# Gated linear attention and a spatial-gating MLP on one core: a new order table, constants as separate operations, more choice of engine

## The chip, the cores and the metric

The kernel runs on one NeuronCore of a Trainium2 chip. A core has a matrix engine (PE, with its weight loads shown as PEld), a vector engine (DVE), a scalar engine (ACT), a general engine (POOL), and a sync engine (SP) that here issues nearly all DMAs. Each engine takes its instructions strictly in the order in which they were written for it, and waits at semaphores for the others. The metric is the device time of one execution in microseconds.

## The reference

```python
def _attn_ref(q, k, v, alpha):                 # each (4, 8, 768, 48)
    state = np.zeros((B, H, D, D)); y = np.zeros_like(q)
    for t in range(S):
        state = alpha[:, :, t, :, None] * state + np.einsum('bhd,bhe->bhde', k[:, :, t], v[:, :, t])
        y[:, :, t] = np.einsum('bhd,bhde->bhe', q[:, :, t], state)

def _moe_ref(x, w_in, w_spatial, b_spatial, w_out):   # x (4, 768, 384)
    h = np.maximum(x @ w_in, 0.0)                     # 384 -> 1024
    u, v = h[..., :512], h[..., 512:]
    v_n = (v - mean(v)) / np.sqrt(var(v) + 1e-06)     # over the last axis
    v_s = np.einsum('ts,bsd->btd', w_spatial, v_n) + b_spatial[None, :, None]
    return (u * v_s) @ w_out                          # 512 -> 384
```

A recurrence over 768 steps for 4 x 8 heads, and behind it an MLP whose gate mixes the 768 positions. All inputs and the output are fp32.

## The kernel before, in words

**The recurrence in chunks.** The 768 steps of each of 4 batch rows are cut into 6 chunks of 128, 24 chunks in all, numbered i = 0 to 23. In a chunk the recurrence becomes matmuls: the logarithm of alpha (`ln`, written to the tile `la`) is summed along time by a matmul with a triangle of ones (`cum`), exponentials of the sum and of its negative (`eexp`, `einv`) scale q and k (`qt`, `kt`), both are transposed on PE (`trk`) and copied out of PSUM (`ev`, tile `kqT`), scores are a matmul (`sc`), masked on DVE (`m`, tile `ptm`), and the output `y` is the masked scores times v (cast to bf16 by `vb`) plus q times the state so far. The state is carried by `upd` (a matmul), `z` (added on DVE), `S` (scaled on POOL) and `sb` (cast to bf16). Chunks 0 to 7 are handled as four pairs, j = 0 to 3, with the same steps under the names `lnp`, `cump`, `einvp`, `eexpp`, `ktp`, `qtp`, `vbp`, `tr`, `updq`, `ya`; a pair's loads are 384 KB each, a single chunk's 192 KB. Then y is cast (`xs`), transposed (`xt`) and copied into `xT` (`xe`).

**The MLP.** For each batch row: `v` (24 groups of three 512-column matmuls, with ReLU on ACT), statistics (`bn`, `rs`) and the normalised `vn`; `u` (32 groups of three 384-column matmuls); `s`, the spatial mixing (32 groups of six, in two parts `mm/0` and `mm/1`), whose copy out of PSUM on DVE adds the bias (`vsb`); `g`, the product with u on POOL or DVE; `o`, the output projection (four matmuls of 384 columns), its copy on ACT, and the store `st`. The last `o` is cut into two column halves (`oh`). The weights come in over 768 KB loads (`w_in/1`, `w_in/0`, `w_sp/0..2`, `w_out`) and are cast to bf16; w_spatial is transposed on PE (`wt`, copied out by `we`). The bias row is spread over 128 partitions by a matmul with a row of ones (`bb`, copied out by `be` into `bsp_bc`). The very last `s` group adds its bias inside the accumulation instead, by a one-row matmul (L957 to L959).

**What sets the order.** Each step is an `Op` with its engine or a choice of engines. Nothing is scheduled at build time: the table `PLAN` (L57) is a list of words such as `D46`, an engine letter and the number of an op, and `replay` (L111) emits the ops in that order. As every engine is a queue in program order, the table fixes each engine's sequence and, where an op allows several engines, which one does it.

**Filler.** A word such as `P53:512:512:192` also orders matmuls on a tile of constants, `junk`, of so many columns each, into the next PSUM bank, just ahead of op 53 on PE (L185 to L189). Their results are overwritten. Each shows as two matmul records. The table of before holds 1,216 columns ahead of the first `cump`, then 464, 304, 304, 172, 148, 228, 240 and 196 up to the first `u` group, and 300 ahead of `wt/2`.

**Constants.** Triangles, masks, the identity, and zeroed paddings of the operand tiles are made by four ops: `consts` (L238 to L265, listed under POOL, though its memsets run on DVE too) and `cz` 0 to 2 (L267). DVE's first instruction is the memset of `junk`; POOL's first is the DMA of the bias row (L1101), then the triangles `le_pair` and `lt_pair`, the identity, and the mask `mask2`. `mask4` and `ut_ones` come later.

**Loads.** SP issues in the table's order: ac/0, kc/0, qc/0, ac/2, vc/0, kc/2, qc/2, vc/2, ac/4, w_in/1, kc/4, qc/4, vc/4, w_in/0, and so on (`ac` is alpha, the number the first chunk). Three pair-sized buffers for each tensor let loads run ahead. Two stores stand ahead of the last load in this queue, the rest behind.

The lines that the steps below touch are in the functions printed here.

Of the kernel before, what the change touches and what calls it, by code (L numbers as in the profile page):

```python
# [36 lines left out]
class Slot:  # L37
# [5 lines left out]
    "kt": {"POOL": 0.9},  # L43
    "vb": {"POOL": 0.48, "ACT": 0.42},
# [6 lines left out]
    "o": {"ACT": 0.4},  # L51
# [6 lines left out]
S34 Q35 S36 Q37 G32 G0 Q33 S38 Q39 S94 Q95 S40 Q41 A42 P53:512:512:192 A54 D1 D2 D56 P43 S96 Q97 S98 Q99 S100 Q101  # L58
S163 Q164 S4 Q5 S165 Q166 S167 Q168 P59:464 G58 G48 A44 A45 A55 D46 D57 D47 P249:304 P49 P61 A50 P51 D52 D60 A62 A102
A250 P71:304 P74 P113 P103 D72 D73 D76 D75 P63 P77:172 D65 A114 D116 P119:148 A104 A64 A115 A105 A78 G66 G67 G106 D107  # L60
D117 D68 P79 P81 P111 P121 P247 P109 G3 G69 A108 A82 A80 D120 D122 D112 D110 P83 A84 A171 D248 S169 Q170 S9 Q10 S307
Q308 P131 P134 D133 D136 D132 D135 G70 G118 P172:228 P182 P123:240 A183 A8 A173 A124 P137 P138 A139 A174 G7 G6 D125
P85 G126 D128 D185 G127 G129 G175 P88 P142 P140 A86 A184 D176 D186 A143 A89 P188 P190 P180 P144 P178 A141 A191 A145
A181 P146 G11 G12 S309 Q310 S311 Q312 D130 D87 D179 D90 D189 P157 A187 A177 A158 A147 A13 P197 P200 P192 D199 D201
D198 D194 D202 P151:196 P155 A315 A193 A91 P326 P316 A327 P203 P153 P204 G195 G196 G329 A317 A328 A318 P149 A205 A154
D159 D156 D152 D330 G319 P208 P334 A209 P206 D320 P332 P324 P210 P322 D92 D335 D325 D333 D148 A207 P212 A211 A150 P347
P215 P221 A213 A160 A222 A216 S14 Q15 P223 P227 S18 Q19 D93 D323 D161 D348 D349 D214 G16 G17 A224 A228 P225 P229 A226
A21 P232 A234 D231 D230 D233 G20 P235:300 P238 S313 Q314 G331 G321 P344 P336 S367 Q368 S369 Q370 S22 Q23 S371 Q372
A237 A236 D217 D162 D346 A240 D338 A239 A218 D219 D220 A375 A337 P251 P263 P259 P376 A377 A378 G339 P264 D345 D341
D265 P260 D261 P255 P252 A380 A25 A24 D381 D253 P256 D257 G340 G342 G379 S409 Q410 S373 Q374 S446 Q447 S411 Q412 S413  # L70
Q414 S415 Q416 S26 Q27 S480 Q481 S448 Q449 S482 Q483 S450 Q451 S484 Q485 P383 A385 A417 S452 Q453 S577 Q578 S486 Q487
S581 Q582 S579 Q580 S583 Q584 P244 P241 P350 A246 D384 D245 D242 D243 P390 P354 P418 D392 D391 A351 A355 G262 G343
A420 A382 G254 G266 P279 P352 P271 P356 P393 P272 A353 A357 A419 G421 A422 A394 P280 P361 P386 P275 P395 A362 A424
A396 A31 D273 D423 D281 D387 P425 D397 D427 D426 D363 G282 G388 P276 P358 D277 P398 G258 G389 G278 G30 A399 A454 A359
A28 A488 P405 P432 P267 P455 P401 A402 A457 A456 D29 P291 P489 P268 A490 A459 D406 D433 D400 D434 D360 P283 P428 D269
D460 A492 D429 D493 G458 G491 P435 A284 A292 A436 G274 G461 G270 G430 G431 S648 Q649 S617 Q618 S650 Q651 S611 Q612
S652 Q653 S613 Q614 S690 Q691 S615 Q616 S694 Q695 S654 Q655 S692 Q693 P287 P462 P437 P495 P403 D463 D464 D497 D496
# [46 lines left out]
def kernel(  # L124
# [12 lines left out]
    nc = tc.nc  # L137
# [93 lines left out]
    def zero_padding(t):  # L231
# [3 lines left out]
        if t.shape[2] > H:  # L235
            nc.vector.memset(flat[:, :, 0::3, 0:D // 2], 0.0)

    def constants(_):  # L238

        nc.vector.memset(junk, 0.5)  # L240
        nc.gpsimd.memset(le_pair, 0.0)
        nc.vector.memset(mask2[:, 0].bitcast(FP32), 0.0)
        zero_padding(lap_bufs[0])
        nc.vector.memset(ones_col, 1.0)
        nc.vector.memset(halves_of, 0.0)
# [911 lines left out]
```

## Time and profile before

| what | value |
|---|---|
| median of 3 runs | 143.13 us (143.12 to 143.7) |
| the profiled execution | 143.08 us |
| its span, first to last instruction | 141.3 us |
| busy: PE, DVE, ACT, POOL | 133.2, 118.3, 108.6, 83.4 us |
| filler on `junk`, all its records | 10.2 us in 24 records |
| DMA | 28.64 MB, mean 203 GB/s |

The span is what the profiler sees between the first and the last instruction; the execution's own time is 1.8 us longer. The busy time of an engine counts its records, which for PE include the filler. A view by stretch cuts the span and gives each engine's busy time in each piece. A view in order of time gives start, length, engine, line, operation, and in brackets how long the engine sat idle before it and who released it. Groups gather instructions of one line and shape, with the mean length of one.

### The profile page before, as it was taken

What the parts mean: (1) busy time and instruction counts of PE and PEld (TensorE: products, weight loads), DVE (VectorE), ACT (ScalarE), POOL (GpSimd) and SP (SyncE); (2) the same over time, 40 slices, a digit from 0 to 9 for tenths busy, and PEclk for the clock granted to TensorE, in tenths of its full rate; (3) what the DMA queues carried; (4) which work ended last, traced back from release to release, by engine and by line L of the source; (5) the groups of instructions that cost most, each with busy time, mean ns of one, the idle gap of its engine ahead of it and who ended that gap; (6) DMA issues with size and microseconds to landing.
All of it is one profiled execution on the core that took longest, in us unless ns stands there. A gap on an engine that the chain in (4) does not pass through costs nothing.

```text
span 141.3 us, 4968 instructions
## 1 busy us (share of the span) xinstructions
PE 133.2 (94%) x1912; PEld 84.2 (60%) x1923; DVE 118.3 (84%) x291; ACT 108.6 (77%) x282; POOL 83.4 (59%) x146
## 2 busy tenths in 40 slices
PE   7989798999999999999999999999999989999990
PEld 3457575575667656565675665656666656566560
DVE  7479878999989599999998898989979779894940
ACT  3677569988989969889887999997889969940061
POOL 6722986293449596982299899500799993000720
PEclk9999999999999999999999999999999999999999
DMA  4999999999898989989799999979978690112044
GB/s 102 323 323 332 331 272 311 225 320 238 241 232 156 283 161 208 205 161 212 154 205 179 193 217 177 222 143 195 250 151 203 225 375 24 70 56 102 0 164 170
DMA packets 89000, 28.64 MB, mean 203 GB/s; under 512 B 83728, under 2 KB 87440, under 8 KB 88976
## 3 DMA queue, kind: packets, MB, share of 16 engines
q1 hardware_dynamic: 88944, 28.32, 81.6%
q8 instruction: 15, 0.25, 0.7%
q14 instruction: 9, 0.07, 0.2%
q0 software_dynamic: 32, 0.00, 0.0%
HBM read 23.60 MB, written 4.72 MB: 200 GB/s over the span
## 4 chain that ended last, share of the span: by engine, by line
PE 71%; DVE 9%; POOL 7%; issue 5%; ACT 4%; ACTq 0%; POOLq 0%; DVEq 0%
PE bank L828 47%; PE bank L187 4%; DVE ptm L594 3%; PE bank L719 2%; PE bank L754 2%; POOL sbd L199 2%; POOL gT L989 2%; PE bank L511 2%; PE bank L782 2%; DVE ptm L765 2%; PE bank L740 1%; PE bank L583 1%; POOL kt L690 1%; PE bank L666 1%; DVE kqT L199 1%
## 5 line engine op out<-in xcount | busy, mean ns | idle before, releaser
L828 PE MATMUL bank<-w_spT,vn 128*128 128x384 bf16 x192 | 36.8, 326 | 0.0
L989 POOL TENSOR_TENSOR gT<-vsb,uT 128x384 bf16<-128x384 f32 x28 | 25.7, 923 | 14.9 <-DVE vsb L976 14.4
L690 POOL TENSOR_TENSOR kt<-kc,binv 128x384 bf16<-128x384 f32 x16 | 14.6, 914 | 13.4 <-ACT bc L685 8.6
L765 DVE TENSOR_TENSOR ptm<-bank,mask 128x512 bf16<-128x512 f32 x32 | 20.7, 682 | 1.9 <-PE bank L398 1.2
L828 PEld LDWEIGHTS <-vn 128*128 128x128 bf16 x192 | 16.6, 97 | 9.5 <-issue 0.2
L976 DVE TENSOR_TENSOR vsb<-bank,bsp_bc 128x384 f32<-128x384 f32 x31 | 16.5, 551 | 4.2 <-PE bank L828 2.5
L828 PE MATMUL bank<-xT,w_in 128*128 128x384 bf16 x96 | 18.7, 326 | 0.0
L828 PE MATMUL bank<-w_out_sb,gT 128*128 128x384 bf16 (+1 forms) x100 | 18.7, 319 | 0.0
L828 PE MATMUL bank<-w_in,xT 128*128 128x512 bf16 x61 | 17.2, 379 | 0.8 <-issue 0.2
L344 POOL TENSOR_TENSOR state<-state,bc 128x192 f32<-128x192 f32 x20 | 10.4, 520 | 11.4 <-DVE state L337 5.4
L197 ACT COPY kqT<-bank 128x512 bf16<-128x512 bf16 x21 | 12.1, 599 | 3.9 <-PE bank L719 1.1
L199 POOL CAST sbd<-state 64x192 bf16<-64x192 f32 x38 | 13.3, 350 | 2.0
L893 DVE BATCH_NORM_STATS2 stats<-v_sb 128x6 f32<-128x512 bf16 x20 | 13.7, 683 | 0.3 <-ACT v_sb L203 0.3
L203 ACT ACTIVATE v_sb<-bank 128x512 bf16<-128x512 f32 x20 | 11.8, 605 | 1.4 <-PE bank L828 1.3
L197 ACT CAST x_sb<-bank 128x384 bf16<-128x384 f32 x24 | 11.4, 490 | 1.5 <-PE bank L623 1.3
L828 PEld LDWEIGHTS <-w_in 128*128 128x128 bf16 x96 | 8.8, 97 | 5.9
L828 PEld LDWEIGHTS <-gT 128*128 128x128 bf16 x100 | 8.9, 97 | 5.6 <-DVE gT L989 0.4
L199 DVE COPY kqT<-bank 128x512 bf16<-128x512 bf16 x27 | 10.5, 416 | 1.9 <-PE bank L511 1.0
L187 PE MATMUL bank<-junk 128*128 128x512 f32 (+9 forms) x24 | 10.2, 529 | 1.1 <-DVE junk L240 1.1
L594 DVE TENSOR_TENSOR ptm<-bank,mask 128x512 bf16<-128x512 f32 x16 | 10.2, 683 | 0.5 <-PE bank L583 0.4
L197 ACT COPY xT<-bank 128x192 bf16<-128x192 bf16 (+1 forms) x26 | 9.4, 379 | 1.6 <-PE bank L398 1.1
L197 ACT COPY o_sb<-bank 128x384 f32<-128x384 f32 x9 | 4.4, 484 | 8.0 <-PE bank L828 8.0
(126 smaller groups left out, 284.0 us busy)
## 6 DMA issues: line engine op xcount, KB each, us to landing
ac<-in_alpha_dram SPq DMA_DIRECT2D x16, 192.0 KB, 4.1
kc<-in_k_dram SPq DMA_DIRECT2D x16, 192.0 KB, 4.8
qc<-in_q_dram SPq DMA_DIRECT2D x16, 192.0 KB, 4.1
vc<-in_v_dram SPq DMA_DIRECT2D x16, 192.0 KB, 3.8
raw_w<-in_moe_w_spatial_dram SPq DMA_DIRECT2D x3, 768.0 KB, 6.8
out_dram<-raw_w SPq DMA_DIRECT2D x11, 192.0 KB, 2.5
out_dram<-o_sb SPq DMA_DIRECT2D x9, 192.0 KB, 1.8
ac<-in_alpha_dram SPq DMA_DIRECT2D x4, 384.0 KB, 5.0
```

The lines of the kernel that those rows point to most:

```text
L187: nc.tensor.matmul(out=flat[:, 0:cols].rearrange("p (a b) -> p a b", a=4), lhsT=junk, rhs=junk[:, None, 0:n].to_broadcast([128, 4, n]), st ...
L197: nc.scalar.copy(out=out, in_=in_)
L199: ENG[eng].tensor_copy(out=out, in_=in_)
L203: nc.scalar.activation(out=out, in_=in_, func=AF.Relu)
L344: ENG[eng].tensor_tensor(out=st["state"], in0=st["state"], in1=st["bc"][:, :, None].to_broadcast([128, HP, D]), op=ALU.mult)
L594: nc.vector.tensor_tensor(out=st[f"ptm{par}"][:, s], in0=st[f"pt{s}{par}"], in1=mask2[:, par], op=ALU.mult)
L690: ENG[eng].tensor_mul(out=k_blocks(kt3)[:, :, :, 0:D], in0=quad(st["kc"]), in1=st["binv"])
L765: nc.vector.tensor_tensor(out=st["ptm"][:, s], in0=st[f"pt{s}"], in1=mask4, op=ALU.mult)
L828: return lambda ps: nc.tensor.matmul(out=out(ps), lhsT=lhsT(), rhs=rhs(), start=start, stop=stop)
L893: nc.vector.bn_stats(out=stats, in_=d["v_sb"][:, tt, :])
L976: nc.vector.tensor_tensor(out=hold["vs"], in0=ps[:, 0:TH], in1=bsp_bc[:, th, :], op=ALU.add)
L989: ENG[eng].tensor_tensor(out=bt[b]["gT"][:, dsl, cols], in0=hold["vs"], in1=bt[b]["uT"][:, dsl, cols], op=ALU.mult)
```

## The change

The order table is replaced as a whole. Around it:

- The four constant ops become separate ones (`c_junk`, `c_la`, `c_kt`, `c_qt`, `c_col`, `c_ut`, `c_id`, `c_m4`, `c_sbd`, `c_row`, `c_half`, `c_tri`, `c_mz`, `c_m2`), each a dependency of the steps that read it. The same tiles are filled by the same kinds of instruction.
- More ops may run on DVE: `kt`, `vb`, `vbp`, `o`, `xs`, and every `g`.
- The last `s` group's bias is added by a matmul of the identity with `bsp_bc`, 128 rows instead of one.

```diff
 ENGINES = {
-    "kt": {"POOL": 0.9},
-    "vb": {"POOL": 0.48, "ACT": 0.42},
+    "kt": {"POOL": 0.9, "DVE": 0.47},
+    "vb": {"POOL": 0.48, "ACT": 0.42, "DVE": 0.27},
...
-    "o": {"ACT": 0.4},
+    "o": {"ACT": 0.4, "DVE": 0.47},
 }
...
 PLAN = """
-S34 Q35 S36 Q37 G32 G0 Q33 S38 Q39 S94 Q95 S40 Q41 A42 P53:512:512:192 A54 D1 D2 D56 P43 S96 Q97 S98 Q99 S100 Q101
-S163 Q164 S4 Q5 S165 Q166 S167 Q168 P59:464 G58 G48 A44 A45 A55 D46 D57 D47 P249:304 P49 P61 A50 P51 D52 D60 A62 A102
...
+S49 Q50 D7 G10 D6 D4 S109 Q110 D3 D15 S51 Q52 D17 G47 Q48 D12 S111 Q112 D0 D2 G16 D5 D13 D1 G9 D11 S53 Q54 A57 G14
+P264:512:512:192 S113 Q114 P68 A265 P58 A117 P262 S55 Q56 D263 A59 P128:436 A69 D61 A60 G71 S115 Q116 P64:512:512:48
+A70 P118 A65 P74 A129 S178 Q179 D72 A119 G131 D62 A130 P76:512:512:204 D75 A77 P66 S19 Q20 G121 D132 A120 D67 D122 G18
+P86:512:512:436 S184 Q185 A63 P136 D88 P134 A73 P126 P124 D87 A137 P89 S182 Q183 A135 D125 P78 D90 A127 D91 S180 Q181
...
+A160 G144 D204 A196 G28 P172 D163 A194 G145 P207 A173 D102 A27 P212 P215 D209 A26 D217 A208 A330 P164:512:480 S33 Q34
...
 """
...
-        op(("xs", i), "ACT", 0.38, xs, got(("y", i), ("xt", i - WK)), prio=P + 9, use=[st["sl_y"]])
+        op(("xs", i), {"ACT": 0.38, "DVE": 0.47}, None, xs, got(("y", i), ("xt", i - WK)), prio=P + 9, use=[st["sl_y"]])
...
-            lambda ps: ps[:, 0:TH], lambda: ones_row, lambda: b_sp_sb[:, th * TH:(th + 1) * TH], True, False))
+            lambda ps: ps[:, 0:TH], lambda: ident, lambda: bsp_bc[:, th, :], True, False))
...
-            op(("g", b, dsl, th), {"POOL": 0.9} if b < B - 1 else {"POOL": 0.9, "DVE": 0.69}, None, gm, got(("s", b, dsl, th)), prio=Q)
+            op(("g", b, dsl, th), {"POOL": 0.9, "DVE": 0.47}, None, gm, got(("s", b, dsl, th)), prio=Q)
...
-    op(("consts",), "POOL", 4.0, constants, prio=-10.0)
-    op(("cz", 0), "DVE", 1.7, zeros(0), prio=-5.0)
-    op(("cz", 1), "DVE", 0.7, zeros(1), prio=-4.0)
-    op(("cz", 2), "POOL", 1.2, zeros(2), [made[("consts",)]], prio=-3.0)
+    op(("c_junk",), "DVE", 0.17, lambda _: nc.vector.memset(junk, 0.5), prio=-20.0)
+    for n in range(2):
+        for x, us, t in (("la", 0.17, lap_bufs[n]), ("kt", 0.49, ktp_bufs[n]), ("qt", 0.17, qtp_bufs[n])):
+            op(("c_" + x, n), "DVE", us, lambda _, t=t: zero_padding(t), prio=-19.0 + 10 * n)
+    op(("c_col",), "DVE", 0.12, c_col, prio=-18.0)
+    op(("c_ut",), "POOL", 0.42, c_ut, prio=-20.0)
+    op(("c_id",), "POOL", 0.5, lambda _: make_identity(nc, ident), prio=-19.0)
+    op(("c_m4",), "POOL", 0.95, c_m4, prio=-8.0 if PAIRS else -18.0)
...
+        op(("c_half",), "DVE", 0.45, c_half, prio=-18.5)
+        op(("c_tri",), "POOL", 1.15, c_tri, got(("c_half",)), prio=-20.5)
+        for par in range(2):
+            op(("c_mz", par), "DVE", 0.25, lambda _, par=par: nc.vector.memset(mask2[:, par].bitcast(FP32), 0.0), prio=-18.2)
+            op(("c_m2", par), "POOL", 1.4, c_m2(par), got(("c_mz", par)), prio=-18.0 + par)
```

In the names of the ops, the new table gives these queues at the start (filler columns in brackets stand ahead of their op; a slash and a number name the pair and its half, or the chunk):

```
PE before  [1216] cump/0/1 cump/0/0 [464] tr/k/0/1 [304] bb/1 tr/k/0/0 tr/q/0/1 tr/q/0/0 [304] sc/0/0 sc/0/1
           cump/1/1 cump/1/0 updq/0 [172] ya/0 [148] tr/k/1/1 xt/0 y/1 ... sc/2/0 sc/2/1 updq/2 [196] u/0/1/0
PE after   [1216] bb/1 cump/0/1 cump/0/0 bb/0 [436] cump/1/1 [1072] tr/k/0/0 cump/1/0 tr/k/0/1 [1228] tr/q/0/1
           tr/q/0/0 [1460] sc/0/0 tr/q/1/1 tr/k/1/1 tr/q/1/0 tr/k/1/0 sc/0/1 updq/0 sc/1/1 sc/1/0 ya/0 cump/2/0
           xt/0 cump/2/1 y/1 updq/1 ya/1 y/2 xt/1 v/0/0 xt/2 v/0/1 ... updq/2 sc/2/0 sc/2/1 [992] u/0/0/0
DVE after  c_col c_qt/1 c_la/1 c_qt/0 c_mz/0 c_mz/1 c_row c_junk c_kt/0 c_kt/1 c_half c_la/0 c_sbd be/0 ktp/0/0
           qtp/0/1 qtp/0/0 ev/k/0/1 qtp/1/1 ev/q/0/0 qtp/1/0 m/0/0/1 m/0/0/0 ev/k/1/0 m/0/1/0 m/0/1/1 z/0
           m/1/1/1 vbp/1/1 m/1/0/0 z/1 m/1/1/0 m/1/0/1 xs/1 cast/w_in/1/1 z/2 xs/2 ...
POOL after c_m4 b_sp c_m2/0 c_id c_tri ktp/0/1 ktp/1/1 ktp/1/0 c_m2/1 S/0 sb/0 ...
ACT after  lnp/0 be/1 lnp/1 einvp/0/0 einvp/0/1 eexpp/0/0 eexpp/0/1 ev/k/0/0 einvp/1/1 einvp/1/0 eexpp/1/1 ...
SP after   ac/0 ac/2 kc/0 kc/2 qc/0 qc/2 vc/0 vc/2 ac/4 w_in/1 vc/4 qc/4 kc/4 w_in/0 ac/6 kc/6 qc/6 w_sp/0 ...
```

No other filler stands in the new table. Up to the first `u` group the same PE ops stand in both tables, in another sequence. Ten stores stand ahead of the last load instead of two. At the end PE's last group is `o/3/4`, 384 columns wide, where it was a half of `o/3/5`.

## The prediction

> **What bounds the kernel now.** I read four views in this order: the engines' totals, busy time by stretch, the first 7 us and the last 4 us in order of time, and the groups with their shapes kept apart. The totals of the page first:
>
> ```profile
> PE 133.2 (94%) x1912; PEld 84.2 (60%) x1923; DVE 118.3 (84%) x291; ACT 108.6 (77%) x282; POOL 83.4 (59%) x146
> PE   7989798999999999999999999999999989999990
> ```
>
> PE is the fullest engine. The stretches tell where it is not full (columns: length, then busy time and count for PE, PEld, DVE, ACT, POOL, the granted clock, the DMA share, GB/s):
>
> ```profile
> 1.05:5.14 4.09, 4.09 (x7) 1.87 (x7) 3.02 (x20) 1.82 (x2) 3.52 (x11) 1.00 0.83 213
> 5.14:16.00 10.86, 9.74 (x167) 6.54 (x165) 8.28 (x18) 7.48 (x17) 4.90 (x11) 1.00 1.14 329
> 16.00:27.46 11.46, 10.15 (x214) 6.99 (x213) 10.14 (x23) 9.71 (x22) 7.61 (x15) 1.00 1.00 279
> 27.46:60.00 32.54, 32.25 (x531) 20.61 (x533) 29.79 (x74) 28.23 (x74) 22.58 (x36) 1.00 0.95 228
> 60.00:100.00 40.00, 39.44 (x562) 25.33 (x565) 36.48 (x92) 36.05 (x104) 24.32 (x41) 1.00 0.96 188
> 100.00:119.77 19.77, 19.27 (x321) 12.40 (x322) 16.89 (x36) 16.98 (x44) 16.45 (x27) 1.00 0.72 207
> 119.77:137.72 17.95, 17.95 (x121) 10.41 (x121) 13.47 (x32) 7.39 (x23) 3.85 (x4) 1.00 0.21 77
> ```
>
> I cut at 27.46 because there PE reaches the first `u` group, and in both order tables exactly the same PE work stands ahead of it. From there to 137.72 PE idles 0.29 + 0.56 + 0.50 + 0 = 1.35 us: this part is PE's own queue. Before it PE idles 1.12 + 1.31 = 2.43 us, and some of its busy time is filler on `junk`. So the time is: PE's start, plus filler, plus real matmuls, plus idle time, plus the end behind PE. The filler's price and the starting points:
>
> ```profile
> 0.83 0.17 DVE L240 MEMSET junk<- 128x128 f32 x1 [0.83 <-PEq L1141]
> 1.05 4.16 PE L187 MATMUL bank<-junk 128*128 128x512 f32 x6 [1.05 <-DVE junk L240]
> 1.22 0.67 POOL L1101 DMA_DIRECT2D b_sp_sb<-in_moe_b_spatial_dram  x1 [0.78 <-POOLq L1141]
> 4.24 0.84 ACT L452 ACTIVATE la<-ac 128x768 bf16<-128x768 f32 x1 [2.22 <-DMA ac<-in_alpha_dram]
> 5.14 0.65 PE L461 MATMUL bank<-la,le_pair 128*128 128x384 bf16 x3
> 5.79 0.94 PE L187 MATMUL bank<-junk 128*128 128x464 f32 x2
> ...
> 137.70 0.70 ACT L197 COPY raw_w<-bank 128x384 f32<-128x384 f32 x2 [0.17 <-PE bank L828]
> 138.63 0.41 SPq L1020 DMA_DIRECT2D out_dram<-raw_w  x1
> ```
>
> ```profile
> L187 PE MATMUL bank<-junk 128*128 128x512 f32 x4 | 3.8, 1101 | 1.1 <-DVE junk L240 1.1
> L187 PE MATMUL bank<-junk 128*128 128x464 f32 x2 | 0.9, 552 | 0.0
> L594 DVE TENSOR_TENSOR ptm<-bank,mask 128x512 bf16<-128x512 f32 x16 | 10.2, 683 | 0.5 <-PE bank L583 0.4
> ```
>
> One filler is two matmul records. The first 1,216 columns run from 1.05 to 5.14, 3.4 ns a column. A later 464-column filler has records of 0.552 us and ends 0.94 us after it starts, so its halves start 0.39 us apart: 0.78 us in all, 1.68 ns a column. The 148- to 300-column ones fit with about 0.1 us on top.
>
> **The change part by part.**
>
> *Filler, up to the first `u`.* Removed: 1,216 + 2,056 columns, 4.09 + 4.15 = 8.24 us (the 2,056 at 1.68, plus 0.7 for eight small ones). So the real work there is 27.46 - 1.05 - 2.43 - 8.24 = 15.7 us. Added: 1,216 columns first, as now 4.1 us, then 436, 1,072, 1,228, 1,460 and 992, together 5,188 at 1.68 = 8.7, plus 0.2 for the 48- and 204-column pieces. That is 13.0 us: **+4.75 us**. No 512-column filler has run at the later pace in this trace; the nearest row is the 464-column one, so I use it, and put 0.3 us on either side. PE takes its queue in order, so the filler is paid whether the operands behind it are there or not. The 300 columns ahead of `wt/2` go later: **-0.6 us** (its record is 0.77).
>
> *The first filler starts later.* `junk` is now DVE's first memset. It comes eighth: ones_col 0.06, three paddings at 0.17, two mask halves at 0.27, ones_row 0.17, eps 0.06, then itself; by the start-to-start distances now (0.11 to 0.27) it ends at 2.15 instead of 1.0. PE starts at 2.2: **+1.15 us**, and the first filler ends at 6.3.
>
> The pace of the first filler is a matter of the clock. The Trainium skill, page "TensorE: Matmul & The Clock Gate", section "What's actually happening", says the gate judges free-running windows of about 3.4 us and the change of pace can come 0.5 us earlier or later. This trace agrees that the pace doubles once (3.4 against 1.68 ns a column, while the granted clock reads 1.00); by the rule the sum below would be 147.0 to 148.0, by the row alone 147.5.
>
> *What is ready at 6.3.* POOL's constants: from 1.22, mask4 0.33 + 0.65, the bias DMA 0.67, two mask2 selects 1.41, ident 0.55, then le_pair and lt_pair 1.25: 6.1 (they were ready at 3.1). PE wants them at 6.5, behind the filler: cost 0; without that cover it would be 1 us, since `lnp/0` ends at 5.1. `c_la/0`, DVE's third last constant, ends at 3.7, before alpha lands at 4.24: 0. The bias row: PE's first real matmul is now `bb/1`, so the whole PE queue waits for this DMA. Issued at 2.25 instead of 1.22, with the 3.5 us to landing of now it is there at 5.75: 0. If it took the 4.9 us that the loads need once the queue is full, 7.15: +0.85. I take the first, its own row.
>
> The Trainium skill, page "DMA: Bandwidth & Descriptors", section "Queues, rings and completion order", says a DMA engine takes turns between its queues packet by packet, so the 16 small packets do not stand behind the loads. The trace's 3.5 us, with loads flowing since 2 us, agrees. By the rule the sum stays 147.5; without it 148.3.
>
> *First loads re-ordered.* Each 384 KB load lands 1.2 us after the one before. kc/0 moves from place 2 to 3 (5.5 to 6.7), qc/0 from 3 to 5 (6.7 to 9.1), vc/0 from 5 to 7 (9.1 to 11.5); ac/2 comes up (7.9 to 5.45). ACT hides this: it now does `be/1` (0.48) and `lnp/1` (0.86) before the first `einvp`, which so starts at 8.0 (now 5.66). `ktp/0/0` can start at 8.45 and `qtp/0/1` at 9.75, after their loads. The same bytes stand ahead of w_in/0, so it lands at 24.15 in both, and its casts are no longer last. Cost 0, apart from the 2.4 us on ACT that the filler covers: PE leaves the 436- and 1,072-column fillers at 10.2, the next at 13.0, the next at 15.9, and each time its operand has been ready for about a microsecond (`ktp/0/0` 9.05, `qtp/0/1` 10.3, `ev/q/0/1` 14.1).
>
> *PE's idle time before the first `u`.* All of the +5.9 can't be additional, as filler takes the place of waiting. Bounds: nothing waits (-2.43) or as much as now (0). From `sc/0/0` at 15.9 I follow the engine that has most queued, DVE: four masks at 0.62 (record 0.683, start to start 0.62), a 0.4 kqT copy, z 0.35, mask, vbp 0.35, mask, z 0.35, two masks end at 23.0, while PE is at `ya/1` by 22.3: 0.7 idle; then `xs/1` 0.55 and the w_in cast 0.46 end at 24.05, `z/2` and `xs/2` at 24.95, each with PE 0.1 to 0.3 early. About 1.2 us idle: **-1.2 us**. The first `u` is then at 27.46 + 1.15 + 4.75 - 1.2 = 32.2.
>
> *From the first `u` to PE's end.* The same matmuls: 110.26 - 1.35 idle - 0.6 filler = 108.3 us. The freer choice moves eight `u`, three `we` and two each of the paired `ktp` and `ev` off DVE and puts seven `o`, five `xs`, two `oh`, two `kt`, two `vb`, two `xe`, one each of `vbp`, `g` and cast on it: by their rows about +3.6 us on DVE (to 122 of some 146, the same 84%), -1 on ACT, -2.5 on POOL. Beside PE that costs 0 on average; single waits I bound by PE's idle time now, 1.35: between -1.1 (nearly none) and +1.7 (about 3 us, the rate of 100.00:119.77 over all of it). I take **0**, because DVE is 90% busy there now and stays so. Eight more stores stand ahead of the last load, 0.5 us each, so vc/22 and vc/23 land about 4 us later; `vb/23` reads its load 6.0 us after landing now, and PE is 4 us later: 0. Without that cover it would be 4 us at the last chunks.
>
> *Last bias and the end.* The bias matmul has 384 columns in both forms (0.331 now, 0.326 for full-row ones), its tile has been there since 10 us: 0. The last PE group is now a full 384-column `o`: copy 0.48 instead of 0.32, store 192 KB (1.86 us to landing now) instead of 96 KB (1.70): **+0.3 us**.
>
> Sum: +1.15 + 4.75 - 1.2 - 0.6 + 0 + 0.3 = +4.4. The profiled execution took 143.08 us (span 141.3 and 1.8 around it), 0.05 below the median of 143.13. Forecast: 143.08 + 4.4 = 147.5 us.
>
> **The rivals.**
>
> - *Waits in the middle.* DVE or ACT falls behind PE's new order and idle time goes to 4 us or more. For it: DVE gets more, and four `g` there take 0.734 each. Against: 99% PE in 27.46:100.00 with DVE at 91%. 150 to 151.5 us.
> - *The bias row holds PE's head.* If it lands after 7.2 us, all behind it moves by 0.85 or more. For it: nothing else can pass `bb/1`. Against: 3.5 us now. 148.3 to 149.3 us, and it shows as PE idle behind the first filler.
> - *No idle time.* The filler swallows all waiting before the first `u` and the middle runs as smoothly as 27.46:60.00: 143.08 + 4.4 - 1.2 - 0.8 = 145.4 us.
> - *The other side: the matmuls get cheaper.* Small row-tiled groups (scores, transposes, updates: some 21 us of PE) pair better in the new mix, so the 108.3 us shrink. Not slower needs -4.4, a fifth of those groups. Against: each group's matmuls stand in the same order inside, and PE follows them back to back now. 143 us and below from that point; 142.3 at a quarter.
>
> **How the numbers follow.** Chances: forecast 0.70, waits in the middle 0.13, bias row 0.08, no idle time 0.05, cheaper matmuls 0.04. Low end: no idle at the start (-1.2) and 1.1 less in the middle, 145.2. High end: idle as now (+1.2) and half of the rival's waits (+1.3), 150.0; above it lie most of the middle rival and a late row on top, 0.14; below lie 0.06. Range 145.2 to 150.0. A measurement of this kernel can tell about 0.5%, 0.7 us, from no change. Slower by more (above 143.85) is all but the last rival, 0.96; of that 0.02 each go to within 0.5% and to faster.
>
> **What would show it.** PE's first filler at 2.2; `la`'s cumulative matmuls at 6.5 (now 5.14); filler records of 0.85 us per 512 columns; the first `u` near 32.2; 108 to 110 us from there to PE's end near 142; no load as the releaser of a wait after 30 us. Wrong would make it: the first `u` before 30.5, filler below 0.7 us per 512 columns, or less than 106 us behind it.

## The result: 4.8% slower, outside the forecast's range

| what | before | after |
|---|---|---|
| median | 143.41 us (143.12 to 144.26, 4 executions) | 151.70 us (150.21 to 154.12, 4 executions) |
| the profiled execution, and its span | 143.08, 141.3 us | 150.21, 148.4 us |
| busy PE, DVE, ACT, POOL | 133.2, 118.3, 108.6, 83.4 us | 138.3, 125.0, 108.4, 83.6 us |
| TensorE's first record, first `u`, last end | 1.05, 27.46, 137.99 us | 2.20, 32.23, 145.07 us |
| from the first `u` to TensorE's end | 110.53 us | 112.84 us |

The ratio is 1.0481, 95% interval 1.0393 to 1.0569 (executions over 1.5% above the fastest of their kernel count in medians and ranges here, but not in ratios). The forecast was 147.5 us with a range up to 150.0, so even the profiled execution, the shortest of the four, lies outside. The page's totals after:

```profile
PE 138.3 (93%) x1915; PEld 85.7 (58%) x1929; DVE 125.0 (84%) x299; ACT 108.4 (73%) x278; POOL 83.6 (56%) x142
PE   4999979999989999999999999899997999999990
DMA  4999998529399998989899999989999011042045
```

The DMA row of the kernel before:

```profile
DMA  4999999999898989989799999979978690112044
```

PE's row is nearly as full as before. What is new is in the DMA row: a hole in the eighth to eleventh slices (5, 2, 9, 3), and then 8s and 9s up to the 31st slice, 115 us. The stretches, cut at the end of the first filler, where `sc/0/0` comes up, and at the first `u` (columns as in the prediction):

```profile
2.20:6.62 4.42, 4.42 (x7) 1.92 (x7) 1.91 (x12) 0.84 (x1) 3.02 (x10) 1.00 1.12 299
6.62:16.80 10.18, 10.18 (x47) 5.17 (x47) 4.09 (x8) 6.28 (x14) 3.97 (x5) 1.00 1.14 334
16.80:32.23 15.43, 14.28 (x340) 9.80 (x341) 14.78 (x32) 12.92 (x28) 8.84 (x19) 1.00 0.79 232
32.23:60.00 27.77, 27.02 (x443) 17.43 (x445) 26.50 (x59) 23.11 (x61) 18.88 (x31) 1.00 0.90 219
60.00:100.00 40.00, 38.74 (x598) 24.62 (x603) 37.80 (x93) 35.93 (x102) 26.03 (x43) 1.00 0.97 195
100.00:119.77 19.77, 18.66 (x252) 11.68 (x253) 17.81 (x42) 15.10 (x41) 12.29 (x19) 1.00 0.74 181
119.77:145.07 25.30, 24.96 (x240) 15.11 (x240) 20.76 (x49) 12.47 (x32) 8.95 (x12) 1.00 0.24 88
```

Up to 32.23 this profile is as forecast: PE starts at 2.20, is never idle until `sc/0/0`, then idle for 15.43 - 14.28 = 1.15 us, and reaches the first `u` at 32.23 (forecast 32.2). Behind it PE idles 0.75 + 1.26 + 1.11 + 0.34 = 3.46 us; before it was 1.35. The next two views tell on what. First the longest waits behind the start that a load ended, and SyncE's own two at its w_spatial loads (us in total, times, longest):

```profile
POOL w_row L200 <- DMA raw_w<-in_moe_w_spatial_dram: 1.8, 1, 1.8
POOL vb L200 <- DMA vc<-in_v_dram: 1.7, 1, 1.7
ACT vb L198 <- DMA vc<-in_v_dram: 1.6, 2, 1.2
...
SPq L1084 <- ACT w_in L198: 5.8, 1, 5.8
SPq L1084 <- POOL w_row L200: 5.6, 1, 5.6
```

SyncE waits 5.8 us before it can issue `w_sp/1`, because the two raw weight buffers are taken until `w_in/0` has been cast, and 5.6 us before `w_sp/2`. It takes its queue in order, so what stands behind them waits too: from 24.75 to 38.20 it issues five DMAs, and that is the hole in the DMA row. The chain of work near 111 us shows a late load on TensorE's path (start, length, what):

```profile
104.07 0.99 SPq L1037
...
105.59 5.52 DMA vc<-in_v_dram
...
111.18 0.04 ACT vb L198
...
111.60 0.60 ACT v_sb L204
...
112.24 0.65 PE bank L819 x3
```

A store is issued, then qc/22 and vc/21, which lands at 111.11; ScalarE casts it at 111.18 (it had been idle for 1.2 us), only then copies the `v` group out of PSUM, and TensorE, which had waited 0.99 us for that bank, goes on. Set beside each other for every load, landing and first use give the picture of the whole kernel, here some rows from the middle (times worked out from the issue order and the records that read the tile; slack taken before rounding):

| load, in SyncE's order | issued | landed | first used | slack |
|---|---|---|---|---|
| vc/13 | 66.42 | 70.21 | 70.33 | 0.12 |
| qc/13 | 67.56 | 71.16 | 75.53 | 4.36 |
| qc/17 | 68.34 | 73.25 | 87.67 | 14.41 |
| ac/15 | 69.20 | 73.96 | 75.53 | 1.57 |
| qc/16 | 73.14 | 76.95 | 89.02 | 12.07 |
| ac/16 | 75.21 | 79.06 | 80.05 | 0.98 |
| vc/19 | 79.00 | 83.51 | 98.19 | 14.68 |
| vc/15 | 80.07 | 84.29 | 84.79 | 0.50 |
| vc/17 | 85.36 | 90.00 | 90.02 | 0.02 |

Loads with 12 to 15 us to spare stand ahead of loads that land as they are needed. Behind 30 us, seven loads of the changed kernel land less than 1 us ahead of their first use; of the kernel before, two do, and its vc/13 has 7.1 us and its vc/17 3.8. The kernel before is not free of such pairs: its ac/23, with 19.2 us to spare, stands three places ahead of vc/18, which has 0.1.

### The profile page after: what moved, and what is told of

Read it like the earlier page. It is cut to its first block, busy times and chain, and to the rows that moved or that the text cites. A ratio compares the mean times of both kernels' runs of the same rounds, so it can differ in the third digit from the quotient of the medians.

```text
span 148.4 us, 4955 instructions
## 1 busy us (share of the span) xinstructions
PE 138.3 (93%) x1915; PEld 85.7 (58%) x1929; DVE 125.0 (84%) x299; ACT 108.4 (73%) x278; POOL 83.6 (56%) x142
## 2 busy tenths in 40 slices
DMA packets 89000, 28.64 MB, mean 193 GB/s; under 512 B 83728, under 2 KB 87440, under 8 KB 88976
## 4 chain that ended last, share of the span: by engine, by line
PE 67%; DVE 15%; ACT 7%; DMA 4%; issue 3%; SPq 2%; ACTq 0%; DVEq 0%
PE bank L819 37%; PE bank L188 9%; DMA vc<-in_v_dram 4%; PE bank L745 2%; PE bank L710 2%; DVE vn L916 2%; ACT v_sb L204 2%; PE bank L731 2%; DVE ptm L585 2%; PE bank L773 2%; PE bank L657 2%; PE bank L502 1%; DVE kqT L200 1%; PE bank L544 1%; DVE ptm L756 1%
## 5 line engine op out<-in xcount | busy, mean ns | idle before, releaser
L819 PE MATMUL bank<-w_spT,vn 128*128 128x384 bf16 x192 | 35.9, 326 | 1.0 <-ACT v_sb L204 1.0
L980 POOL TENSOR_TENSOR gT<-vsb,uT 128x384 bf16<-128x384 f32 x27 | 25.1, 947 | 14.9 <-DVE vsb L967 14.4
L819 PEld LDWEIGHTS <-vn 128*128 128x128 bf16 x192 | 17.3, 97 | 11.5 <-issue 1.2
L819 PE MATMUL bank<-xT,w_in 128*128 128x384 bf16 x96 | 19.2, 326 | 0.2 <-ACT uT L204 0.2
L681 POOL TENSOR_TENSOR kt<-kc,binv 128x384 bf16<-128x384 f32 x14 | 12.9, 930 | 10.4 <-ACT binv L669 9.6
L198 ACT COPY kqT<-bank 128x512 bf16<-128x512 bf16 x23 | 13.0, 595 | 5.6 <-PE bank L502 4.4
L188 PE MATMUL bank<-junk 128*128 128x512 f32 (+5 forms) x30 | 14.3, 616 | 2.2 <-DVE junk L1050 2.2
L200 DVE COPY kqT<-bank 128x512 bf16<-128x512 bf16 x25 | 9.9, 412 | 2.9 <-PE bank L502 1.9
L916 DVE TENSOR_SCALAR vn<-v_sb,mvs,rstd 128x512 bf16<-128x512 bf16 x24 | 11.0, 489 | 1.6 <-ACT rstd L909 1.6
L204 ACT ACTIVATE uT<-bank 128x384 bf16<-128x384 f32 x22 | 10.5, 496 | 2.1 <-PE bank L819 2.0
L198 ACT CAST x_sb<-bank 128x384 bf16<-128x384 f32 x19 | 8.9, 481 | 3.5 <-PE bank L773 2.1
```

What stands on the lines that cost most here:

```text
L188: nc.tensor.matmul(out=flat[:, 0:cols].rearrange("p (a b) -> p a b", a=4), lhsT=junk, rhs=junk[:, None, 0:n].to_broadcast([128, 4, n]), st ...
L198: nc.scalar.copy(out=out, in_=in_)
L200: ENG[eng].tensor_copy(out=out, in_=in_)
L204: nc.scalar.activation(out=out, in_=in_, func=AF.Relu)
L681: ENG[eng].tensor_mul(out=k_blocks(kt3)[:, :, :, 0:D], in0=quad(st["kc"]), in1=st["binv"])
L819: return lambda ps: nc.tensor.matmul(out=out(ps), lhsT=lhsT(), rhs=rhs(), start=start, stop=stop)
```

## The experiments

Filler columns feed no output; where a kernel leaves some out, nothing else of the computation changes. SyncE's order is given by the names of the ops.

### What the start costs

**Only the first filler left.**

```diff
-P128:436 ... P64:512:512:48 ... P76:512:512:204 ... P86:512:512:436 ... P164:512:480
+P128 ... P64 ... P76 ... P86 ... P164
```

> The changed kernel with only its first filler (1,216 columns); the other 5,188 columns are left out, nothing of the computation is. Theory S (the filler and the late start cost the 4.8 us ahead of the first u group): PE then waits for operands instead, the first u comes at about 28.5 us instead of 32.2 and the time falls by 3 to 4.5 us, to 146 to 147. Rival W (the operands set the start, the filler only fills): the first u stays at 31 or later and the time within 1 us of 150.2. Rival C (PE's clock halves when the filler is gone): matmul starts 0.32 us apart instead of 0.16 per 384 columns somewhere before 28 us, time about 150.

Measured: 147.18 us (146.41 to 148.34), ratio 1.0278 [1.0221, 1.0334], a little above the range of theory S; the rival of the clock happened in part. The first `u` is at 28.67. So 5,188 columns, 8.7 us of PE by the 1.68 ns of the prediction, were worth 3.6 us at the first `u`: without them PE waits more, and the granted clock falls to 0.84 in 16 to 27 us. From the first `u` to PE's end it now takes 113.46 us, and 15 loads land less than 1 us ahead of use.

**The kernel before with 2,880 more columns ahead of `ya/0`.**

```diff
-P77:172
+P77:172:512:512:512:512:512:320
```

> The kernel before with 2,880 columns of filler more, ahead of ya/0 (at 12.1 us). At 1.68 ns a column that is 4.85 us. If a late start is passed on one to one: first u at 32.3, time 143.1 + 4.85 = 148.0, idle time behind it 1.4 us as before. If a late start by itself brings the 3 us that the changed kernel loses behind its first u (the load queue waiting for buffers): 150 to 151, and loads are the releasers of waits after 60 us.

Measured: 147.57 us (147.56 to 147.92), ratio 1.0304 [1.0277, 1.033]. The first `u` moves from 27.46 to 32.36, 4.90 us for 2,880 x 1.68 ns = 4.84: the pace of 1.68 ns holds for pieces of 512 too. Behind it:

```profile
32.36:60.00 27.64, 27.50 (x443) 17.56 (x442) 25.16 (x62) 23.45 (x62) 17.81 (x29) 1.00 0.97 224
60.00:100.00 40.00, 39.83 (x610) 25.23 (x608) 36.60 (x92) 36.39 (x104) 28.12 (x47) 1.00 0.94 184
```

PE idles 0.14 and 0.17 us, and from the first `u` to its end it takes 110.49 us, as before (110.53). This is what decides it: the kernel before, started as late as the changed one, loses nothing behind the first `u`. The changed kernel's extra loss there comes with the new order, not from a late start alone.

**The memset of `junk` first on VectorE.**

```diff
-S49 Q50 D7 G10 D6 D4 S109 Q110 D3 D15 S51 Q52 D17 G47 Q48 D12 S111 Q112 D0 D2
+S49 Q50 D0 D7 G10 D6 D4 S109 Q110 D3 D15 S51 Q52 D17 G47 Q48 D12 S111 Q112 D2
```

> The changed kernel with the memset of junk as DVE's first instruction. Theory S: PE starts at 1.05, the first filler ends at 5.2, the bias row (issued at 1.72, 3.5 us) and the triangles (5.6) are just there, the first u comes at 31.1 and the time falls by 1.1 us to 149.1. Rival (bias row or triangles hold PE's head, so the late start cost nothing): first u at 32.0 or later, time within 0.4 us of 150.2.

Measured: 150.07 us (149.45 to 150.78), ratio 1.0474 [1.0431, 1.0516]. The first `u` comes at 31.41, 0.82 us earlier than in the profile without the edit, but PE ends at 145.01 (145.07 without). That would say that something other than PE's queue sets the pace behind the first `u`, but it is not shown by this run: a second profile of the unaltered kernel (further down) has its first `u` at 31.51 and PE's end at 146.06, so the unaltered kernel differs from itself by as much.

### SyncE's order

**Loads ahead of the blocked weights.**

```diff
 SP: w_sp/0
-    w_sp/1 vc/6 ac/8 w_sp/2 kc/8 qc/8 ac/9 vc/8 vc/9
+    vc/6 ac/8 kc/8 qc/8 w_sp/1 ac/9 vc/8 vc/9 w_sp/2
     qc/9 ac/10 ...
```

> The changed kernel with seven loads moved ahead of the w_spatial loads that wait for a raw buffer: vc/6, ac/8, kc/8, qc/8 ahead of w_sp/1, and ac/9, vc/8, vc/9 ahead of w_sp/2. Theory L (the sync queue stands behind w_sp/1 and w_sp/2 while the DMA engines run empty, and the load stream never catches up): the DMA share between 27 and 31 us rises to 0.9 or more, the waits on vc and qc loads after 60 us go, the time falls by 1.5 to 3 us to 147.2 to 148.7. Rival D (DVE's longer list makes the 3 us): within 0.7 us of 150.2, the first u still at 32.2 in either case.

Measured: 149.79 us (149.36 to 150.46), ratio 1.045 [1.0402, 1.0498], above the range of theory L. Three instead of seven loads land less than 1 us ahead of use, and the spread of the executions shrinks, but the profiled execution has the same span as without the edit, 148.4: vc/21 still lands at 111.03, behind the stores. The edit gives most loads of the middle 2 to 4 us more slack and leaves the end as it was.

**The ten stores behind the last loads.**

```diff
 SP: ... qc/23
-    st/0/3 st/0/1 qc/19 qc/21 st/1/4 ac/23 kc/19 st/1/5 qc/20 st/1/1 st/0/5 kc/22 st/0/4
-    qc/22 vc/21 ac/22 kc/23 st/1/0 st/0/0 st/1/3 vc/23 vc/22
+    qc/19 qc/21 ac/23 kc/19 qc/20 kc/22 qc/22 vc/21 ac/22 kc/23 vc/23 vc/22
+    st/0/3 st/0/1 st/1/4 st/1/5 st/1/1 st/0/5 st/0/4 st/1/0 st/0/0 st/1/3
```

> The changed kernel with the ten stores that stand between qc/23 and vc/23 in SyncE's order moved behind vc/22, nothing else. Theory Q (the stores hold the last loads back: SyncE stood 2.3 us at a store whose tile VectorE had still to write, and vc/21 landed at 111.1, 0.1 us before its use): vc/21 lands 4 to 7 us earlier, the 1.0 us gap of TensorE at 111.3 goes, and the time falls by 0.7 to 1.2 us, to 149.0 to 149.5. Theory V (VectorE is full from 88 to 98 us and sets the pace there): vc/21 lands earlier all the same, but the time falls by 0.5 at most, 149.7 to 150.2. If the ten stores fill the queue behind vc/22, the tail can lengthen by some 0.5.

Measured: 151.55 us (149.67 to 152.18), ratio 1.0484 [1.0408, 1.0559]. The gap at 111 us is gone and 111.97 us lie between the first `u` and PE's end, but ten loads land less than 1 us ahead of use, all of them before 95 us, and the time is as scattered. By itself this says nothing about the time.

**Both.**

> The changed kernel with both edits of SyncE's order: seven loads ahead of w_sp/1 and w_sp/2, and the ten stores behind vc/22. Theory Q (loads set the 2.3 us behind the first u): no load lands less than 1.5 us ahead of its use behind 40 us, and the time falls by 1.5 to 2.3, to 147.9 to 148.7. Theory V (VectorE, partly stopped by GpSimd, sets them): 149.2 to 149.8, with the jump of 0.9 us between 88 and 96 us still there.

Measured: 149.03 us (148.64 to 149.43), ratio 1.0384 [1.0337, 1.0432]; 111.43 us behind the first `u`, and no load lands less than 1.8 us ahead of its use behind 30 us. That lies between the ranges of the two theories, and it was measured on another chip than the changed kernel. So both were put side by side:

> The changed kernel itself, unaltered, to stand on the same chip and in the same rounds as the next one. Theory Q (loads that land at the moment of their use make its time large and scattered): median 150.5 to 152, range 2 us or more. If its first four times were chance: median 149.5 to 150.3 with a range under 1 us.

> The changed kernel with both edits of SyncE's order (seven loads ahead of w_sp/1 and w_sp/2, ten stores behind vc/22), a second time, beside the unaltered one. Theory Q: 148.6 to 149.4 again, range under 1.2 us, 1.5 to 2.5 us below the unaltered kernel of the same rounds. If queue order is not the cause: within 0.7 us of it.

Measured: the unaltered changed kernel 151.78 us (151.22 to 153.43), ratio 1.0615 [1.0566, 1.0664]; with both queue edits 148.93 (148.06 to 151.97), 1.0373 [1.0341, 1.0405]. The order of one queue is worth 2.85 us between the medians (3.0 without the longest execution with the edits). One of the six executions with the edits took 151.97, so the range that I expected for it did not hold. The stretches from the first `u` on, unaltered:

```profile
31.51:60.00 28.49, 27.69 (x446) 17.64 (x448) 27.23 (x60) 23.81 (x64) 19.59 (x32) 1.00 0.85 204
60.00:100.00 40.00, 37.40 (x576) 23.62 (x579) 36.15 (x87) 34.00 (x94) 25.19 (x42) 1.00 0.97 195
100.00:119.77 19.77, 19.00 (x259) 11.69 (x259) 18.25 (x44) 15.45 (x43) 11.36 (x18) 1.00 0.81 196
```

and with both edits:

```profile
32.22:60.00 27.78, 27.02 (x443) 17.42 (x445) 26.50 (x59) 23.12 (x61) 18.87 (x31) 1.00 0.94 218
60.00:100.00 40.00, 38.94 (x599) 24.78 (x605) 37.79 (x94) 36.33 (x102) 25.81 (x43) 1.00 0.99 193
100.00:119.77 19.77, 19.66 (x289) 12.44 (x289) 18.91 (x44) 16.08 (x43) 13.13 (x21) 1.00 0.56 161
```

PE's idle time falls from 2.60 to 1.06 us in the middle stretch and from 0.77 to 0.11 in the last one.

What these two edits do not tell is whether the wait at the weights alone makes the loads late. The kernel before with 2,880 more columns speaks against it: SyncE waits 6.3 us at its `w_sp/1`, longer than here (though 1.8 at `w_sp/2`, not 5.6), its DMA row has a hole too, and one load of it lands within 1 us of its use:

```profile
SPq L1081 <- ACT w_in L197: 6.3, 1, 6.3
SPq L1081 <- POOL w_row L199: 1.8, 1, 1.8
...
DMA  4999989919899998979899898989995392023034
```

That leaves the sequence of the loads themselves, and it was tried alone, with the waits and the stores left in place.

**The loads in the order of their first use.**

```diff
 SP (loads of chunk 8 and later, among their own places; w_sp, w_out and stores unmoved):
-    ... vc/14 kc/14 kc/13 vc/13 qc/13 qc/17 ac/15 kc/15 qc/14 qc/16 qc/15 ac/16 ac/17 ac/19 kc/16 vc/19 vc/15 ac/18 ...
+    ... vc/13 vc/14 kc/13 qc/13 ac/15 kc/14 qc/14 qc/15 kc/15 ac/16 ac/17 ac/19 vc/15 ac/18 qc/17 kc/16 qc/16 ...
-    ... vc/17 ac/21 vc/18 kc/18 ac/20 vc/20 kc/21 kc/20 qc/23 st/0/3 st/0/1 qc/19 qc/21 st/1/4 ac/23 kc/19 ...
+    ... vc/17 qc/18 kc/18 vc/18 vc/19 ac/20 ac/21 kc/19 qc/20 kc/21 qc/21 st/0/3 st/0/1 qc/19 kc/20 st/1/4 vc/20 ...
```

> The changed kernel with the loads of ac, kc, qc and vc from chunk 8 on put in the order of their first use, among their own places in SyncE's queue; w_sp/1, w_sp/2, w_out and all stores stay where they are. Behind 30 us the changed kernel's profiled execution has loads that land 10 to 17 us ahead of use (qc/17, vc/19, qc/23) standing ahead of loads that land at the moment of use (vc/13, vc/17, kc/18). Theory Q1 (the wait at w_sp/1 and w_sp/2 alone makes the loads late): 151 to 152 as the unaltered kernel, with late loads as many. Theory Q2 (it is as much the sequence of the loads): fewer than 4 loads land under 1 us ahead of use, 149 to 150.3, 111.3 to 112.2 us from the first u to TensorE's end, and a smaller scatter.

Measured: 148.88 us (148.38 to 149.09, 5 executions), ratio 1.0372 [1.0343, 1.0402]: as much as both other edits together (1.0373), and below the range that I gave. It was measured on another chip than the changed kernel, so the ratios to the kernel before are what can be compared: 1.0481 and 1.0615 without the edit. The waits at the weights are there as before, and so is the hole in the DMA row:

```profile
SPq L1084 <- ACT w_in L198: 5.9, 1, 5.9
SPq L1084 <- POOL w_row L200: 5.6, 1, 5.6
...
DMA  4999999619399897999979998998989111042045
```

```profile
32.54:60.00 27.46, 26.81 (x445) 17.31 (x444) 26.05 (x58) 22.80 (x60) 18.44 (x30) 1.00 0.90 212
60.00:100.00 40.00, 39.50 (x606) 24.70 (x605) 37.83 (x94) 36.28 (x103) 26.16 (x43) 1.00 1.01 202
100.00:119.77 19.77, 19.77 (x277) 12.36 (x279) 18.91 (x45) 16.08 (x43) 12.76 (x20) 1.00 0.77 191
```

So the lateness needs both, this sequence and the lack of slack that the waits and the stores leave; more slack (loads ahead, stores behind) or a better sequence mend it alike:

| kernel | loads that land under 1 us ahead of use, behind 30 us | first `u` to PE's end |
|---|---|---|
| before | 2 | 110.53 us |
| before, 2,880 columns more | 1 | 110.49 us |
| changed | 7 | 112.84 us |
| changed, the second time | 16 | 114.55 us |
| changed, `junk` first | 13 | 113.60 us |
| loads ahead only | 3 | 112.66 us |
| stores behind only | 10 | 111.97 us |
| loads ahead, stores behind | 0 | 111.43 us |
| the same, the second time | 0 | 111.37 us |
| loads by first use | 2 | 111.41 us |

The count goes with the loss, but not strictly: ten late loads before 95 us cost less than three near the end. The two profiled executions of one and the same changed kernel differ by 1.7 us here, and in the number of late loads. That lateness also makes the scatter is likely, not shown: with no slack, a load that is some tenths late can delay TensorE, and with that the freeing of the buffers that the next loads need. The six executions of the second time lie between 151.2 and 153.4 us, the five with the loads by first use between 148.4 and 149.1; with both queue edits five lie between 148.1 and 149.2 and one at 152.0.

### The choice of engines

**The kernel before's engine for every operation, in the new order** (110 words change their letter).

> The changed kernel's order with the kernel before's choice of engine for all 110 operations that the two give to different engines. Theory E (the choice of engines costs: VectorE 125.0 us busy against 118.3): VectorE's busy time falls to 119 to 121, and of the 2.3 us lost behind the first u 1 to 2 come back: 148.2 to 149.2. Theory O (the order was made for these engines, and is worse with others): 150.5 to 153, with new waits of TensorE for ScalarE. Theory Q of the loads: 150 to 150.5, as the landing times stay.

Measured: 157.73 us (156.86 to 158.16), ratio 1.0992 [1.0942, 1.1043]. VectorE's busy time falls to 119.8 us as expected, and the time rises by 6 us: the first `u` is at 35.48, and 117.08 us lie behind it, with three loads under 1 us ahead of use. That is above the range of every theory. The new order goes badly with the old engines; the cost of the choice alone can't be read from this.

**Two operations of VectorE out of GpSimd's way.** The trace of the changed kernel has VectorE operations that read and write SBUF only and that last up to three times as long as the same operation elsewhere:

```profile
71.04 0.40 DVE L916 TENSOR_SCALAR vn<-v_sb,mvs,rstd 128x512 bf16<-128x512 bf16 x1
...
93.10 1.13 DVE L916 TENSOR_SCALAR vn<-v_sb,mvs,rstd 128x512 bf16<-128x512 bf16 x1
```

```profile
93.17 0.91 POOL L681 TENSOR_TENSOR kt<-kc,binv 128x384 bf16<-128x384 f32 x1 [0.34 <-DMA kc<-in_k_dram]
```

The `vn` of 1.13 us stands beside GpSimd's `kt` of 0.91. Four of the 24 `vn` last 0.59 to 1.13 us and all four lie beside a GpSimd operation (six others that do are not lengthened); in the kernel before all 24 last 0.38 to 0.41. The groups, before and after:

```profile
L925 DVE TENSOR_SCALAR vn<-v_sb,mvs,rstd 128x512 bf16<-128x512 bf16 x24 | 9.1, 402 | 0.5 <-ACT rstd L918 0.4
L916 DVE TENSOR_SCALAR vn<-v_sb,mvs,rstd 128x512 bf16<-128x512 bf16 x24 | 11.0, 489 | 1.6 <-ACT rstd L909 1.6
```

```diff
-... A700 D758 ...      -... D662 A735 P792 A573 D767 P736 A793 D768
+... A700 G758 ...      +... A735 P792 A573 D767 P736 A793 D768 D662
```

> The changed kernel with two words changed: vb/16 on GpSimd in place of VectorE (808 ns there beside GpSimd's kt and gT, 345 for the same cast elsewhere), and vn/2/1 two operations later on VectorE (1131 ns beside GpSimd's kt, 402 for one without). Theory V: the 1.2 us of VectorE between 88 and 98 us are saved, each vn takes 405 to 420 ns there, and the time falls by 0.4 to 1.0, to 149.2 to 149.8. Theory Q (the loads set the end at 111 us): VectorE saves as much, but the time stays at 150.0 to 150.4.

Measured: 152.09 us (150.35 to 153.83), ratio 1.0527 [1.0454, 1.06]. Inconclusive: the scatter is larger than what was to be seen (20 loads of the profiled execution land less than 1 us ahead of use). Therefore once more on top of both queue edits:

> The changed kernel with the two edits of SyncE's order (seven loads ahead of w_sp/1 and w_sp/2, ten stores behind vc/22), which took 149.03, and with vb/16 on GpSimd and vn/2/1 two operations later on VectorE. Theory V (what is left behind the first u, 0.7 us between 88 and 96 us, is VectorE's, 1.2 us of it stopped by GpSimd): 148.2 to 148.6. Theory N (that loss has another cause, or is made good in a later wait): 148.8 to 149.3.

Measured: 149.83 us (148.65 to 151.11), ratio 1.0409 [1.0353, 1.0466]; not below the same kernel without it. The `vn` in question is back to 0.40:

```profile
96.32 0.40 DVE L916 TENSOR_SCALAR vn<-v_sb,mvs,rstd 128x512 bf16<-128x512 bf16 x1
```

and from the first `u` (at 34.03) to PE's end it takes 111.23 us in place of 111.43. The stops are real, 1.2 us of VectorE at this place; in these profiles taking them away is worth 0.2 us behind the first `u`. So they are not the main cause of the loss there. Whether the rest of VectorE's longer list costs something was not tried by itself.

### Small parts

**The last bias row alone, in the kernel before.**

```diff
-lambda ps: ps[:, 0:TH], lambda: ones_row, lambda: b_sp_sb[:, th * TH:(th + 1) * TH], True, False))
+lambda ps: ps[:, 0:TH], lambda: ident, lambda: bsp_bc[:, th, :], True, False))
```

> The kernel before with the last bias row put in by the changed kernel's one 128-row matmul (ident and the spread bias) in place of the one-row matmul, nothing else. The prediction costed it at nothing: 143.0 to 143.7 and a ratio of 0.998 to 1.003. The rival: a full-row matmul that shortens or lengthens the chain of the last group by more than 0.3 us would show as a ratio outside this.

Measured: ratio 1.000 [0.9976, 1.0025]. It costs nothing.

**The kernel before without its later filler** (all fillers but the first).

> The kernel before with only its first filler (1,216 columns) and the other 2,356 columns left out (no output depends on them). Theory F (filler ahead of a ready matmul costs its own length, about 4 us at 1.68 ns a column less what the matmuls would have waited for anyway): the first u comes 1 to 3 us earlier and the time falls to 140.5 to 142.3. The rival, the granted clock: fewer columns let it fall, and the slower matmuls take the gain back: 142.8 to 144.

Measured: 144.96 us (144.36 to 146.39), ratio 1.0107 [1.006, 1.0154]: slower, though PE has some 4 us less of filler (2,356 columns at 1.68 ns), and above the range of either theory. The first `u` comes at 28.64; with the filler it came at 27.46, and at 28.24 in the profile of the last bias row above, which has the same start. The granted clock had fallen:

```profile
PEclk9999559999999999999999999999999999999999
...
20.00:21.00 1.00, 1.00 (x58) 1.00 (x56) 0.65 (x2) 1.00 (x3) 0.00 (x0) 0.50 0.67 203
```

It was 0.50 from about 14 to 21 us. The other executions go with it: three with a mean clock of 0.973 to 0.976 took 144.4 to 144.5 us, three with 0.952 or 0.953 took 145.4 to 146.4. The rival that I had named is the one that happened, and it took back more than the gain: this filler earns its place.

### Filler and queue together

**Both queue edits, the two moves of VectorE, and only the first filler.**

> The same with all filler columns behind the first 1,216 left out as well (they feed nothing; no output depends on them). If filler and queue order cost independently, the 3 to 4.5 us that the filler cost in the changed kernel come off once more: 144.6 to 145.6. If with the earlier start the loads are late again, 146 to 147, with VectorE, ScalarE or GpSimd waiting for loads of vc, kc or qc in the waits.

Measured: 145.52 us (144.3 to 146.26), ratio 1.0128 [1.0078, 1.0178], inside the first range. But the first `u` is at 27.23, and 113.17 us lie behind it: GpSimd waits 7.2 us for `w_sp/1` and `w_sp/2`, which now come too late for a PE that is 5 us earlier, and PE waits for GpSimd's casts of them. So with `w_sp/1` and `w_sp/2` moved up again:

> The changed order with only the first 1,216 filler columns, the ten stores behind vc/22, vb/16 on GpSimd, vn/2/1 two operations later, and w_sp/1 behind vc/6 and ac/8 only, w_sp/2 behind kc/8, qc/8, ac/9 and vc/8: in the run of all edits GpSimd had waited 7.2 us for w_sp/1 and w_sp/2 and TensorE 2.1 us for GpSimd's casts of them. If those waits were what that run had lost behind the first u (113.2 us against 111.3 to 111.4 with the filler): 143.4 to 144.6, about the kernel before. If the loads of kc, qc and vc come late again instead: 145 to 146.5.

Measured: 144.82 us (144.15 to 146.74), ratio 1.0086 [1.0052, 1.012], between the two ranges; the first `u` at 27.69, 112.25 us behind it, and six loads within 1 us of their use. With the loads in the order of first use as well:

> The kernel with only the first 1,216 filler columns and both parts of SyncE's order undone, which took 144.82, and with the loads in the order of need as well. It had six loads landing under 1 us ahead of use. If these cost what is left behind the first u: 143.3 to 144.3, about the kernel before, with 111 to 111.6 us behind the first u (112.25 without). If what is left is GpSimd's wait for the w_spatial loads and the order of TensorE's work: 144.4 to 145.2.

Measured: 143.86 us (142.96 to 145.63, 12 executions), ratio 1.0031 [1.0004, 1.0058]; the first `u` at 27.09, 111.86 us behind it, no load behind 30 us with less than 2.6 us of slack. The rest of the new order, with its filler cut and SyncE's queue put in order (loads by need, `w_sp` and stores moved), is within 0.6% of the kernel before. Of the 5 to 6% between the two kernels these two parts of the change account for all but some 0.3, the two moves of VectorE counted in. No version here beats the kernel before.

## Why the prediction was wrong, step by step

- *PE starts later*: 2.20 as forecast. *Bias row at PE's head*: `bb/1` started at 6.55, when the filler was through; the term 0 was right in both profiles, in the second by little: the row landed at 5.68 and `bb/1` started at 5.84.
- *Filler up to the first `u`, idle time before it*: the fillers ended 0.7 to 0.9 us later than forecast (10.9, 13.8 and 16.8), idle time was 1.15 (forecast 1.2), and the first `u` came at 32.23 (32.2). So an error of 0.9 was made good by another between `sc/0/0` and the first `u`, which is luck. In the second profile the fillers ended within 0.2 us of the forecast and the first `u` came at 31.51: the first filler alone took 4.42 us in the one profile and 3.71 in the other (forecast 4.1). The price of the filler itself is confirmed from outside by 4.90 us for 2,880 columns.
- *The end*: +0.3 forecast, next to nothing found: 3.36 us between PE's end and the last store's, 3.30 before.
- *Last bias*: 0 forecast, ratio 1.000 measured by itself.
- ***From the first `u` to PE's end*: the step that failed.** I took 0, that is 110.53 less the 0.6 of the removed filler, 109.9 us (the prediction cut at 137.72; PE's last record ends at 137.99); the profiled executions show 112.84 and 114.55, 2.9 and 4.6 more, beyond the bound of +1.7 that I had put on single waits. Two sentences of that step carried it. "`vb/23` reads its load 6.0 us after landing now, and PE is 4 us later: 0" looked at the last load alone: vc/21 stands behind seven of the ten stores and had 7.9 us of slack before; it has 0.1 now, while vc/23 itself kept 8.9. And "no load as the releaser of a wait after 30 us" was set down without comparing, load by load, the new sequence of SyncE with the new sequence of use. For the first loads I had done that ("first loads re-ordered"), for the later ones I had not; DVE I followed operation by operation, SyncE from 30 us on only by its stores. Put in the order of use, the same loads leave 111.41 us, 1.4 and 3.1 us less than those two profiles; side by side on one chip, the two queue edits bring back 2.85 us of the whole time.
- *The rivals*: "waits in the middle, 150 to 151.5 us" comes nearest, with a chance of 0.13: PE idles 3.46 and 4.51 us behind the first `u` in the two profiles, and the medians are 151.7 and 151.8. But it came by another engine than I named: not DVE or ACT falling behind, but loads that landed late. I had checked that rival with the engines' shares, where a late load doesn't show. DVE's added work I put at 3.6 us; it was 6.7, as operations lengthened beside GpSimd came on top (`vn` alone 1.9 us).
- *The sum, with the loads mended*: 148.88 us beside 143.23, +5.7, where the sum of the other steps was +4.4. Some 0.9 us of the difference lie behind the first `u` (111.41 against 110.53), 0.6 more against the 109.9 of the forecast. Here the term for the matmuls was itself too small. These profiles hold the same number of matmul records behind the first `u`, but for two of filler: the kernel before with 2,880 more columns is busy there for 109.84 us (1,540 records) of 110.49, the changed one with both queue edits for 110.10 us (1,538) of 111.43, and with the loads by first use for 110.08 (1,538) of 111.41. With the 0.77 us of the two filler records taken off, PE is 1.0 us longer busy and 0.7 us longer idle in the new order, so "the same matmuls" did not cost the same in another sequence. Two gaps of 0.2 and 0.4 us at the transposes of w_spatial near 42 us can be seen; what causes the rest stays open.

## What to carry to other kernels

An in-order DMA queue is to be checked against the order of use: for every load, landing and first use, before and after; a load with 15 us to spare ahead of one with none can be a loss that no engine's share shows. By and large the kernels with many such loads here are also those that lost behind the first `u`; the count alone doesn't give the size. Filler is paid at its full length where operands are ready (4.90 us for 2,880 columns), but not all of it is waste: in the kernel before, with the later filler left out, the granted clock fell to 0.50 for 6.8 us and the kernel was 1.1% slower. And one profile is not enough where the time scatters: the changed kernel's two profiles differ by 1.7 us behind the first `u`.

## What the runs showed of the hardware

- Some VectorE operations between SBUF tiles are held up beside GpSimd's: `vn` takes 0.40 us elsewhere, 1.13 beside a `kt` of 0.91, and 0.40 again where it was moved away. The Trainium skill, page "SBUF — State Buffer", section "Who interferes with whom", says that the two engines share a pair of SBUF ports which one of them holds for a whole instruction. This trace agrees in that all four lengthened `vn` end 0.14 to 0.15 us behind the end of a GpSimd operation. Which of the two is held it doesn't settle: the `vn` at 93.10 starts 0.07 us ahead of `kt` and is held, another at 37.09 starts 0.6 us into a GpSimd cast and takes 0.40.
- The granted clock can halve without a long pause of TensorE: in the kernel before without its later filler it was 0.50 from about 14 to 21 us, and the longest gap between matmul records from 5 to 21 us was 1.02 us. The Trainium skill, page "TensorE: Matmul & The Clock Gate", section "Why this matters for your kernels", warns of pauses above about 3 us; here it took less than that, with TensorE 64 to 80% busy in the 6 us ahead of the fall.
- Leaving filler out doesn't always bring the clock down: in the runs with only the first filler in the new order the profiled executions show a mean clock of 0.988, 1.00, 0.988 and 1.00. Over all 26 executions of these four kernels it lay between 0.965 and 1.00, and at 0.996 or above in 8.
